# An MLP whose work is ordered by a list scheduler written in the kernel, in place of the framework's scheduler

## The chip, the cores and the metric

The kernel runs on one core of a Trainium2 chip. The metric is the device time of one launch in microseconds (us), median of the runs.

## What is computed

Sigmoid attention over 4 batches of 12 heads (448 tokens, 64 channels), then two MLP layers over all 1792 tokens (768 channels, 2048 hidden); weights arrive as 64-bit floats.

```python
scores = scale * np.matmul(q, k.transpose(0, 1, 3, 2)) - np.log(S)
attn = 1.0 / (1.0 + np.exp(-scores))
x = np.matmul(attn, v)               # to [1792, 768]
h = x @ w_in;  r = np.maximum(h, 0.0);  x = (r * r) @ w_out
h = x @ w_in2; x = (np.maximum(h, 0.0) + alpha * np.minimum(h, 0.0)) @ w_out2
```

## The kernel before

After the attention, the MLP runs as 32 **units** `(layer, p, fp)`: two layers, two pairs of batches (896 tokens), eight pairs of 128 hidden channels. Every fp32 operand is split into a high and a low part, and three matmuls (high-high, high-low, low-high) make one product.

A unit has an inward half and an outward half. Inward, seven products in Winograd's way (`product`, line 389; 9 matmuls of 448 columns each, so 63) go to three PSUM banks `h0` to `h2`, in the order 0, 1, 2, 1, 2, 0, 1. Products 3, 4 and 6 add on to a bank whose earlier sum VectorE must have read (`add`, line 581, into tiles `c12`, `c22`, `c21`). ScalarE and VectorE then make the hidden values `g` (`hidden`, line 397: squared ReLU in layer 0, leaky ReLU in layer 1). Outward (`out_products`, line 435), six pairs of outputs in layer 0 or seven in layer 1, with 12 matmuls each, 72 of 448 or 84 of 384 columns, go in turn to two double banks `o0` and `o1`; `collect` (line 457) adds each pair to `acc` on VectorE (line 468; ScalarE at line 466 where `fp` is 0). A pair needs the bank of the pair before the last.

Beside this, each unit prepares the next ones. For the weights, `load` brings a 64-bit block to one of two `raw` buffers, `scale` (ScalarE, lines 94 and 96) and `join` (VectorE, line 103) make a 32-bit one in `words_i` or `words_o`, or in place, which is also kept in DRAM (line 105) and recalled for the second pair of batches (line 111). `weight_sum` and `weight_parts` make the inward operands `wi`; `out_parts` and `out_low` (ScalarE line 494, GpSimd line 498) make the outward operands `wo` from `words_o`, of which there is one buffer. For the other pair of batches, `x_sums` and `wait_in_dram` prepare its inputs on GpSimd through one buffer `stage`, which a DMA empties to DRAM (line 504).

The attention stands in `tc.manual_schedule()`, which keeps the program's order. The MLP stands behind it. There, the program only says at which step a job is put (`at("i0", ...)`), and the framework's scheduler orders all engines by its own estimates, TensorE too. Each engine executes its queue in order.

Of the kernel before, what the change touches and what calls it, by code (L numbers as in the profile page):

```python
# [16 lines left out]
P = 128  # L17


@with_exitstack  # L20
def fused_kernel(ctx: ExitStack, tc: tile.TileContext, q, k, v, w1i, w1o, w2i, w2o, alpha, out):
# [14 lines left out]
    nc = tc.nc  # L36
# [33 lines left out]
    words = {kind: wpool.tile([P, 2, DM], F32, name=f"words_{kind}") for kind in "io"}  # L70
    late = dpool.tile([P, NC * PAIR], F32, name="late")
# [4 lines left out]
    raws = {}  # L76

    def load(n, kind, j):
# [4 lines left out]
        raw = raws[n, kind, j] = wpool.tile([P, DM, 2], I32, tag="raw", name=f"raw{n}{kind}{j}", bufs=2)  # L83
        d = raw.rearrange("p m t -> p (m t)").bitcast(I64)
# [5 lines left out]
    def scale(n, kind, j, word):  # L90

        half = raws[n, kind, j][:, :, word]
# [5 lines left out]
    def join(n, kind, j):  # L98

        raw = raws.pop((n, kind, j))  # L100
        layer, p, fp = UNITS[n]
        to = words[kind][:, j].bitcast(I32) if layer == 0 else raw.rearrange("p m t -> p (m t)")[:, :DM]
        nc.vector.scalar_tensor_tensor(out=to, in0=raw[:, :, 1], scalar=3, in1=raw[:, :, 0], op0=ALU.logical_shift_left, op1=ALU.bitwise_or)
        keep = kept[layer, 2 * fp + j, kind] = dpool.tile([P, DM], F32, name=f"kept{n}{kind}{j}")
        nc.sync.dma_start(out=keep, in_=to.bitcast(F32))

    def recall(n, kind):

        layer, p, fp = UNITS[n]
        for j in range(2):  # L110
            nc.sync.dma_start(out=words[kind][:, j], in_=kept[layer, 2 * fp + j, kind])

    def turn_of(n):

        return n if n < NB else n + NB

    def weight_sum(i, eng=None):
# [3 lines left out]
        eng = eng or nc.vector  # L121
# [10 lines left out]
    def weight_parts(what):  # L132

        first, w = {"a1": (0, words["i"][:, 0]), "a2": (2, words["i"][:, 1, HALF:]), "s12": (3, sums[:, :2 * HALF]), "s34": (5, sums[:, 2 * HALF:])}[what]
        hi, lo = (W[:, i, first * HALF:first * HALF + w.shape[-1]] for i in range(2))
        nc.scalar.activation(hi, w, AF.Copy)  # L136
        nc.vector.tensor_sub(lo, w, hi)  # L137
# [6 lines left out]
    def blocks(p):  # L144
        a = values_of(p)
        return ([a[:, kh * KH + c, t] for c in range(KH)] for kh, t in ((0, 0), (0, 1), (1, 0), (1, 1)))

    def x_sums(p, i, c, eng):
        b11, b12, b21, b22 = blocks(p)
        to, x, y = ((b12, b12, b11), (b12, b22, b12), (b11, b12, b11), (b12, b21, b12))[i]  # L150
        eng.tensor_sub(to[c], x[c], y[c])  # L151


    def x_parts(p, i, c, eng, to=None):
        b11, b12, b21, b22 = blocks(p)
        x = (b11, b12, b12, b11, b22, b21, b12)[i][c]
        hi, lo = to or (X[i][:, 0, c], X[i][:, 1, c])
        nc.scalar.activation(hi, x, AF.Copy)  # L158
        eng.tensor_sub(lo, x, hi)  # L159
# [4 lines left out]
    with tc.manual_schedule():  # L164
# [6 lines left out]
        with tc.tile_pool(name="apool", bufs=1) as apool, tc.tile_pool(name="apsum", bufs=1, space=bass.MemoryType.PSUM) as psum:  # L171
# [139 lines left out]

            ready_x = []
            for what in X_ORDER[:-1]:
                make = x_sums if what[0] == "s" else x_parts
                ready_x += [lambda i=int(what[1]), c=c, make=make: make(0, i, c, either()) for c in range(KH)]
            for d in range(ND):
# [17 lines left out]
                if d in (2, 3):  # L334
                    load(*early[d - 2])
                if item:
                    scale(*item, 1)
                    scale(*item, 0)
# [15 lines left out]
                if item:  # L354
                    join(*item)
                if 0 <= i < 4:
                    load(*early[i + 2])
# [14 lines left out]
    mpool = ctx.enter_context(tc.tile_pool(name="mpool", bufs=1, reuse_waits="tile"))  # L372
    psum = ctx.enter_context(tc.tile_pool(name="mpsum", bufs=1, space=bass.MemoryType.PSUM, reuse_waits="tile"))
    X.append(mpool.tile([P, 2, KH, S], F32R, name="x6"))
    e21, e22, e12, e11 = (mpool.tile([P, S], F32, name=f"c{s}") for s in ("21", "22", "12", "11"))
    pos = [mpool.tile([P, S], F32, name=f"pos{i}") for i in range(2)]
    WO = [mpool.tile([P, 2, DM], F32R, name=f"wo{j}") for j in range(2)]
    G = [mpool.tile([P, 2, PAIR], F32R, name=f"g{j}") for j in range(2)]
    acc.append(mpool.tile([P, NC * PAIR], F32, name="acc1"))
    stage = mpool.tile([P, 2, S], F32R, name="stage")  # L380
    two = [psum.tile([P, 2, 512], F32, name="o0")]
    hb = [psum.tile([P, 512], F32, name=f"h{i}") for i in range(3)]
    two.append(psum.tile([P, 2, 512], F32, name="o1"))
    BANK = (0, 1, 2, 1, 2, 0, 1)
    OPERAND = (0, 4, 3, 5, 6, 1, 2)
    HIGH, LOW = ((0, 0), (0, 1)), ((1, 0),)
    turns = {"pair": 0, "pos": 0, "x": 0}

    def product(k):

        ps = hb[BANK[k]][:, :S]
        for c in range(KH):
            at = OPERAND[k] * HALF + c * P
            for i, (wp, xp) in enumerate(((0, 0), (0, 1), (1, 0))):
                nc.tensor.matmul(ps, W[:, wp, at:at + P], X[k][:, xp, c], start=(k < 3 and c == 0 and i == 0), stop=(c == KH - 1 and i == 2), skip_group_check=True)  # L395

    def hidden(n, src, e, j, t):

        layer, p, fp = UNITS[n]
        gh, gl = (G[j][:, i, t * S:(t + 1) * S] for i in range(2))  # L400
        if layer == 0:
            nc.scalar.activation(e, src, AF.Relu)  # L402
            nc.scalar.activation(gh, e, AF.Square)  # L403
            nc.scalar.activation(e, e, AF.Square)  # L404
            second = lambda: None
        else:
            f = 2 * fp + j
            up = pos[turns["pos"] % 2]
            turns["pos"] += 1
            nc.scalar.activation(up, src, AF.Relu)  # L410
            nc.scalar.activation(e, src, AF.Relu, scale=-1.0)  # L411

            def second():
                nc.vector.scalar_tensor_tensor(out=e, in0=e, scalar=nal[:, f:f + 1], in1=up, op0=ALU.mult, op1=ALU.add)  # L414
                nc.scalar.activation(gh, e, AF.Copy)  # L415
        return second, lambda: nc.vector.tensor_sub(gl, e, gh)  # L416

    def outputs(n):

        if UNITS[n][0] == 0:  # L420
            return [[(c, t), (c + 1, t)] for t in (1, 0) for c in range(0, NC, 2)]
        return [[(m, 0), (m, 1)] for m in reversed(range(NM))]

    def out_product(n, o, ps, j, ways, begin, end):

        for i, (gi, wi) in enumerate(ways):
            if UNITS[n][0] == 0:
                c, t = o
# [223 lines left out]
```

## Time and profile before

| | |
|---|---|
| median of 3 runs | 1110.5 us (1109.63 to 1111.69) |
| the profiled execution, own time | 1106.94 us |
| its span, first to last instruction | 1105.2 us |
| TensorE busy, matmul / weight load | 1057.4 us (96%) / 911.7 us (82%) |
| VectorE, ScalarE, GpSimd busy | 764.2, 587.4, 271.6 us |
| mean granted TensorE clock | 0.993 |

PE is TensorE's matmuls, PEld its weight loads, DVE VectorE, ACT ScalarE, POOL GpSimd, SP the queue that issues DMAs. Matmuls overlap: one lasts 0.36 us in the records while the next starts 0.2 us after it. Idle time before an instruction, and what ended it, stands in brackets in a timeline.

### The profile page before, as it was taken

The page shows a single profiled execution, that of the slowest core. Times are in us where ns is not written, and L with a number is a line of the kernel's source. Part 1 is how long each engine was busy: PE and PEld are TensorE (multiplying, and loading weights), DVE is VectorE, ACT ScalarE, POOL GpSimd, SP SyncE. Part 2 cuts the span into 40 slices and gives each one's busy share as a digit, 9 for nine tenths or more (in the row PEclk, how much of TensorE's full clock was granted, in tenths as well). Part 3 has the DMA queues.
Part 4 walks back from the last instruction along what each step waited for, and adds up shares of the span by engine and source line. Part 5 has one row for each costly group of instructions (what it writes and reads, how often), then busy time and mean ns, then how long its engine had stood idle before and what let it go on. Part 6 is the DMA issues. An engine that isn't in the chain of part 4 may idle for free.

```text
span 1105.2 us, 14871 instructions
## 1 busy us (share of the span) xinstructions
PE 1057.4 (96%) x5607; PEld 911.7 (82%) x5607; DVE 764.2 (69%) x990; ACT 587.4 (53%) x933; POOL 271.6 (25%) x229
## 2 busy tenths in 40 slices
PE   9999899999999989999999989899999999999998
PEld 5555458888888878887889878899999999999997
DVE  5556967677777785777677674666666756666664
ACT  4567667665555667666656435433333553333332
POOL 0011224354311151543211156411111211111110
PEclk9999899999999999999999999999999999999999
DMA  7577827456654677687766533322112922121103
GB/s 151 143 196 197 238 85 269 172 197 221 221 172 156 229 272 247 236 272 239 250 227 214 217 142 111 126 72 60 58 59 56 334 71 59 58 58 59 57 26 101
DMA packets 126008, 174.79 MB, mean 158 GB/s; under 512 B 55536, under 2 KB 98800, under 8 KB 124272
## 3 DMA queue, kind: packets, MB, share of 16 engines
q1 hardware_dynamic: 123440, 172.59, 48.6%
q10 hardware_dynamic: 2496, 1.25, 0.4%
q8 instruction: 44, 0.72, 0.3%
q14 instruction: 28, 0.23, 0.1%
HBM read 123.87 MB, written 49.94 MB: 157 GB/s over the span
## 4 chain that ended last, share of the span: by engine, by line
PE 52%; issue 13%; DMA 11%; ACT 10%; POOL 8%; DVE 5%; SPq 0%; ACTq 0%; POOLq 0%; DVEq 0%
PE o L433 24%; PE h L395 18%; PE av L265 4%; POOL wo L498 4%; PE sc L245 3%; DMA kept_x<-stage 3%; POOL stage L159 2%; ACT wi L136 1%; POOL acc L151 1%; POOL x L159 1%; ACT c L404 1%; ACT c L402 1%; DVE acc L468 1%; ACT g L403 1%; PE scr L255 1%
## 5 line engine op out<-in xcount | busy, mean ns | idle before, releaser
L395 PE MATMUL h<-x,wi 128*128 128x448 f32 x2016 | 429.4, 368 | 16.8 <-DVE c L581 12.5
L395 PEld LDWEIGHTS h<-x,wi 128*128 128x128 f32 x2016 | 376.3, 188 | 59.3 <-DVE c L581 19.0
L433 PE MATMUL o<-g,wo 128*128 128x448 f32 x1152 | 245.0, 369 | 14.4 <-DVE acc L468 11.8
L498 POOL TENSOR_TENSOR wo<-words_o,wo 128x384 fp32r<-128x384 f32 x128 | 138.7, 1115 | 461.9 <-ACT wo L494 461.9
L433 PEld LDWEIGHTS o<-g,wo 128*128 128x128 f32 x1152 | 214.8, 189 | 41.1 <-DVE acc L468 19.0
L433 PE MATMUL o<-wo,g 128*128 128x384 f32 x1344 | 241.6, 337 | 7.1 <-ACT g L415 5.8
L433 PEld LDWEIGHTS o<-wo,g 128*128 128x128 f32 x1344 | 235.1, 189 | 10.9 <-ACT g L415 6.6
L468 DVE TENSOR_TENSOR acc<-o,acc 128x768 f32<-128x768 f32 (+1 forms) x182 | 184.2, 1015 | 58.0 <-PE o L433 57.2
L581 DVE TENSOR_TENSOR c<-h,c 128x448 f32<-128x448 f32 x160 | 99.1, 620 | 108.3 <-PE h L395 96.3
L494 ACT ACTIVATE wo<-words_o 128x768 fp32r<-128x768 f32 x64 | 51.0, 838 | 168.7 <-PE o L433 132.5
L416 DVE TENSOR_TENSOR g<-c,g 128x448 fp32r<-128x448 f32 x128 | 80.5, 644 | 30.6 <-ACT c L404 29.4
L247 ACT ACTIVATE a<-sc,bias 128x896 f32<-128x896 f32 x72 | 69.1, 1003 | 32.1 <-PE av L265 19.2
L159 POOL TENSOR_TENSOR stage<-acc,stage 128x448 fp32r<-128x448 f32 x36 | 48.1, 1335 | 150.7 <-ACT stage L158 150.7
L136 ACT ACTIVATE wi<-sums 128x768 fp32r<-128x768 f32 x64 | 53.6, 839 | 44.9 <-PE h L395 44.7
L137 DVE TENSOR_TENSOR wi<-sums,wi 128x768 fp32r<-128x768 f32 x64 | 69.0, 1081 | 7.4 <-ACT wi L136 6.5
L137 DVE TENSOR_TENSOR wi<-words_i,wi 128x768 fp32r<-128x768 f32 x64 | 52.5, 830 | 14.5 <-ACT wi L136 14.5
L151 POOL TENSOR_TENSOR acc<-acc 128x448 f32<-128x448 f32 x40 | 59.2, 1485 | 12.0 <-DVE acc L468 5.8
L265 PE MATMUL av<-a,v 128*64 128x448 f32 x288 | 61.7, 565 | 0.0
L158 ACT ACTIVATE stage<-acc 128x448 fp32r<-128x448 f32 x36 | 20.7, 574 | 66.3 <-DMA kept_x<-stage 53.2
L414 DVE SCALAR_TENSOR_TENSOR c<-c,nal,pos 128x448 f32<-128x448 f32 x64 | 43.5, 680 | 8.8 <-ACT c L411 8.6
L402 ACT ACTIVATE c<-c 128x448 f32<-128x448 f32 x48 | 27.3, 569 | 38.6 <-DVE c L581 38.6
L159 POOL TENSOR_TENSOR x<-acc,x 128x448 fp32r<-128x448 f32 x15 | 21.9, 1478 | 102.4 <-ACT x L158 102.4
(166 smaller groups left out, 943.7 us busy)
## 6 DMA issues: line engine op xcount, KB each, us to landing
kept_x<-stage SPq DMA_DIRECT2D x36, 448.0 KB, 3.4
x<-kept_x SPq DMA_DIRECT2D x12, 1344.0 KB, 10.1
v<-in_v_dram SPq DMA_DIRECT2D x24, 192.0 KB, 2.9
nat<-in_q_dram SPq DMA_DIRECT2D x22, 192.0 KB, 4.0
nat<-in_k_dram SPq DMA_DIRECT2D x20, 192.0 KB, 3.6
late<-held SPq DMA_DIRECT2D x12, 224.0 KB, 2.1
acc<-late SPq DMA_DIRECT2D x1, 2688.0 KB, 9.2
out_dram<-acc SPq DMA_DIRECT2D x14, 192.0 KB, 2.9
```

Of the source, the lines that this page charges most:

```text
L136: nc.scalar.activation(hi, w, AF.Copy)
L137: nc.vector.tensor_sub(lo, w, hi)
L151: eng.tensor_sub(to[c], x[c], y[c])
L159: eng.tensor_sub(lo, x, hi)
L247: nc.scalar.activation(sig[u, j], ps[:, :, :S], AF.Sigmoid, bias=bias[:, :1], scale=SCALE)
L265: nc.tensor.matmul(avs[u][h * D:(h + 1) * D, :S], vals[u][:, h, j, :], a[:, h, :], start=(u % 2 == 0 and j == 0), stop=(u % 2 == 1 and j = ...
L395: nc.tensor.matmul(ps, W[:, wp, at:at + P], X[k][:, xp, c], start=(k < 3 and c == 0 and i == 0), stop=(c == KH - 1 and i == 2), skip_group ...
L416: return second, lambda: nc.vector.tensor_sub(gl, e, gh)
L433: nc.tensor.matmul(ps, *ops, start=(begin and i == 0), stop=(end and i == len(ways) - 1), skip_group_check=True)
L468: nc.vector.tensor_add(part, both, part)
L498: nc.gpsimd.tensor_sub(WO[j][:, 1, at], words["o"][:, j, at], WO[j][:, 0, at])
L581: nc.vector.tensor_add(to, hb[bank][:, :S], other)
```

## The change

The whole MLP moves into `manual_schedule()`, and its work is no longer emitted where it is written. Each operation is added to a `Plan` with its engine, a duration, and keys for what it reads and writes. `Plan.run` places the operations in simulated time and emits them by their start. TensorE's operations keep the order in which they were added. Due times run back from TensorE's order; each other engine takes, among the operations that can begin, the one due first, unless it would delay a more urgent one that becomes ready meanwhile. VectorE operations that read two SBUF tiles and GpSimd's (`port=True`) are placed one at a time. DMAs are taken one after the other at 0.28 MB/us with 2 us on top.

The operations, their engines and their number stay as they were. `raw` becomes two fixed tiles, `join` loses its DMA to `keep`, and the recalls are one DMA each.

```diff
+class Plan:
+    HOP = 0.10
+    TAIL = {"PE": 0.17, "DVE": 0.085, "ACT": 0.095, "POOL": 0.04}
...
+    def run(self):
...
+        for j in pe:
+            due[j] = at
+            at += jobs[j][1]
+        for j in reversed(range(n)):
+            late = min((due[s] - self.HOP for s in after[j]), default=at + 50.0) - length(j) - self.TAIL.get(jobs[j][0], 0.0)
+            due[j] = min(due[j], late) if jobs[j][0] == "PE" else late
...
+        def begin(j, t):
+            t = max(t, ready[j])
+            return max(t, port_free) if jobs[j][4] else t
+        def choose(e):
+            queue = waiting[e]
+            if e == "PE":
+                queue = [j for j in queue if j == pe[next_pe]]
...
+            now = sorted((j for j in queue if begin(j, free[e]) <= t + 1e-9), key=lambda j: due[j])
+            soon = [j for j in queue if begin(j, free[e]) > t + 1e-9]
+            for j in now:
+                end = t + jobs[j][1]
+                if not any(due[s] < due[j] and begin(s, free[e]) < end and end > due[s] for s in soon):
+                    return t, j
...
+            if e == "SP" or size:
+                dma_free = max(dma_free, t + 0.1) + size / 0.28e6
+                end = dma_free + 2.0
...
+        for t, j in sorted(order):
+            jobs[j][2]()
...
+        def act(cols): return 0.10 + 0.00083 * cols
+        def dve(cols): return 0.07 + 0.00105 * cols
+        def pool(cols): return 0.13 + 0.0023 * cols
+        PE_IN, PE_OUT = 0.2005, (0.2005, 0.1735)
...
+            add("SP", 0.05, lambda: load(at, n, kind, j), [], [high, low], size=2 * DM * BYTES)
+            add("ACT", act(DM), lambda: scale(at, 1), [high], [high])
+            add("ACT", act(DM), lambda: scale(at, 0), [low], [low])
+            add("DVE", dve(DM), lambda: join(at, n, kind, j), [high, low], to, port=True)
...
-        step(0)
-        nc.scalar.activation(e21, hb[0][:, :S], AF.Copy)
-        do("i0")
...
+            add_inward(n)
...
+            add_outward(n)
+        plan.run()
```

Three places where the order moves. The numbers in names are buffers: in the rows of before `c_1789` is `c12`, `c_1788` `c22`, `c_1787` `c21`; in those of the change they are `c_1784`, `c_1783`, `c_1782`.

VectorE before, end of unit 2 and inward half of unit 3:

```order
L129 TENSOR_TENSOR sums<-words_i,sums 128x384
L468 TENSOR_TENSOR acc_76<-o_1803,acc_76 128x2x448
L103 SCALAR_TENSOR_TENSOR words_o<-raw4o_2469 128x768
L581 TENSOR_TENSOR c_1789<-h_1801,c_1787 128x448
L103 SCALAR_TENSOR_TENSOR words_o<-raw4o_2484 128x768
L581 TENSOR_TENSOR c_1788<-h_1802,c_1787 128x448
L137 TENSOR_TENSOR wi<-sums,wi 128x768
```

The same place in the change:

```order
L202 SCALAR_TENSOR_TENSOR words_o<-raw_82 128x768
L720 TENSOR_TENSOR acc_76<-o_1798,acc_76 128x2x448
L240 TENSOR_TENSOR wi<-words_i,wi 128x384
L202 SCALAR_TENSOR_TENSOR words_o<-raw_81 128x768
L720 TENSOR_TENSOR acc_76<-o_1794,acc_76 128x2x448
L720 TENSOR_TENSOR acc_76<-o_1798,acc_76 128x2x448
L662 TENSOR_TENSOR c_1784<-h_1796,c_1782 128x448
L202 SCALAR_TENSOR_TENSOR words_i<-raw_82 128x768
L662 TENSOR_TENSOR c_1783<-h_1797,c_1782 128x448
```

The two joins into `words_o` leave the inward half for the outward half of the unit before; joins into `words_i`, which nothing on GpSimd reads, stand among the adds.

TensorE before, outward half of unit 1, second and third pair:

```order
L433 MATMUL o_1799<-g_1795,wo_1793 128x448 x6
L433 MATMUL o_1803<-g_1795,wo_1793 128x448 x6
L395 MATMUL h_1800<-x_70,wi 128x448
L433 MATMUL o_1799<-g_1795,wo_1793 128x448 x3
L433 MATMUL o_1799<-g_1796,wo_1794 128x448 x3
```

The same place in the change:

```order
L534 MATMUL o_1794<-g_1790,wo_1788 128x448 x6
L534 MATMUL o_1798<-g_1790,wo_1788 128x448 x6
L534 MATMUL o_1794<-g_1790,wo_1788 128x448 x3
L534 MATMUL o_1794<-g_1791,wo_1789 128x448 x3
L534 MATMUL o_1794<-g_1790,wo_1788 128x448 x3
```

The matmuls of the next unit's first product, one to five per unit, no longer stand between the second and third pair.

ScalarE before, end of unit 16 and inward half of unit 17:

```order
L494 ACTIVATE wo_1793<-words_o 128x768
L466 ACTIVATE acc_76<-o_1799 128x768
L494 ACTIVATE wo_1794<-words_o 128x768
L587 ACTIVATE c_1787<-h_1800 128x448
L158 ACTIVATE stage<-acc_1797 128x448
L136 ACTIVATE wi<-sums 128x768
L158 ACTIVATE stage<-acc_1797 128x448
L410 ACTIVATE pos_1791<-c_1788 128x448
```

The same place in the change:

```order
L628 ACTIVATE wo_1788<-words_o 128x768
L628 ACTIVATE wo_1789<-words_o 128x768
L718 ACTIVATE acc_76<-o_1794 128x768
L669 ACTIVATE c_1782<-h_1795 128x448
L190 ACTIVATE raw_82<-raw_82 128x768
L192 ACTIVATE raw_82<-raw_82 128x768
L261 ACTIVATE stage<-acc_1792 128x448
L236 ACTIVATE wi<-sums 128x768
L650 ACTIVATE pos_1786<-c_1783 128x448
```

One write of `stage` is left in the inward half, ahead of the first hidden value; the next one comes in the outward half.

## Rows read from the trace of the kernel before

**Rows 1.** Stretches: busy us (count) of PE, PEld, DVE, ACT, POOL; clock; DMA share; GB/s.

```profile
164.30:649.10 484.80, 453.63 (x2166) 403.08 (x2165) 358.06 (x429) 290.55 (x475) 157.44 (x121) 1.00 0.65 221
649.10:713.70 64.60, 57.95 (x295) 53.87 (x294) 37.52 (x50) 31.64 (x56) 33.35 (x29) 0.97 0.35 120
713.70:1105.20 391.50, 386.65 (x2057) 368.73 (x2055) 261.46 (x380) 158.94 (x279) 60.31 (x60) 1.00 0.26 82
428.40:431.80 3.40, 3.40 (x10) 2.80 (x10) 2.02 (x3) 3.40 (x6) 0.00 (x0) 0.50 0.49 146
```

**Rows 2.** Lines 395 and 433: ns min/median/max, first and last start in us.

```profile
L395 PEld LDWEIGHTS h<-x,wi x2016: 186/188/338, 164.3 to 1085.4; 128*128 128x128 f32 x184
L395 PE MATMUL h<-x,wi x2016: 360/368/659, 164.3 to 1085.6; 128*128 128x448 f32 x184
...
L433 PE MATMUL o<-wo,g x1344: 333/334/525, 663.3 to 1100.5; 128*128 128x384 f32 x192
```

**Rows 3.** Timeline of PE, a unit of layer 1: start us, us busy.

```profile
952.11 0.56 PE L395 MATMUL h<-x,wi 128*128 128x448 f32 x2
...
979.68 0.57 PE L395 MATMUL h<-x,wi 128*128 128x448 f32 x2
```

**Rows 4.** Timeline of PE, a unit of layer 0.

```profile
317.53 12.77 PE L395 MATMUL h<-x,wi 128*128 128x448 f32 x62
330.14 3.13 PE L433 MATMUL o<-g,wo 128*128 128x448 f32 x14
...
337.56 9.99 PE L433 MATMUL o<-g,wo 128*128 128x448 f32 x48 [0.95 <-DVE acc L468]
347.39 0.97 PE L395 MATMUL h<-x,wi 128*128 128x448 f32 x4
```

**Rows 5.** Waits of PE from 164 us on: total us, times, longest.

```profile
PE h L395 <- DVE c L581: 12.5, 14, 2.1
PE o L433 <- DVE acc L468: 12.3, 14, 2.1
PE o L433 <- ACT g L415: 5.8, 2, 4.3
PE h L395 <- ACT wi L136: 3.5, 3, 2.0
PE o L433 <- DVE g L416: 2.2, 5, 0.8
```

**Rows 6.** Timeline of unit 3, inward half.

```profile
257.98 4.66 POOL L498 TENSOR_TENSOR wo<-words_o,wo 128x384 fp32r<-128x384 f32 x4 [2.41 <-ACT wo L494]
...
260.01 1.76 DVE L103 SCALAR_TENSOR_TENSOR words_o<-raw4o 128x768 int32<-128x768 int32 x1 [1.56 <-POOL wo L498]
...
261.70 0.61 DVE L581 TENSOR_TENSOR c<-h,c 128x448 f32<-128x448 f32 x1
...
262.37 2.09 PE L395 MATMUL h<-x,wi 128*128 128x448 f32 x9 [1.11 <-DVE c L581]
...
265.16 5.75 PE L395 MATMUL h<-x,wi 128*128 128x448 f32 x27 [0.70 <-DVE c L581]
```

**Rows 7.** Timeline of unit 17, ScalarE and PE.

```profile
693.04 0.58 ACT L158 ACTIVATE stage<-acc 128x448 fp32r<-128x448 f32 x1 [7.04 <-DMA kept_x<-stage]
...
697.02 5.31 PE L433 MATMUL o<-wo,g 128*128 128x384 f32 x20 [4.25 <-ACT g L415]
```

**Rows 8.** Timeline of DVE, the unit of rows 3, adds of the first two pairs.

```profile
951.31 1.95 DVE L468 TENSOR_TENSOR acc<-o,acc 128x768 f32<-128x768 f32 x2
```

**Rows 9.** Joins of one unit, and all adds of line 468: ns min/median/max.

```profile
L103 DVE SCALAR_TENSOR_TENSOR words_o<-raw7o x2: 957/1360/1764, 350.2 to 352.9; 128x768 int32<-128x768 int32 x2
...
L468 DVE TENSOR_TENSOR acc<-o,acc x182: 944/958/1092, 213.5 to 1100.9; 128x768 f32<-128x768 f32 x98, 128x896 f32<-128x896 f32 x84
```

**Rows 10.** DMA issues from 180 to 390 us: count, KB each, median us to landing.

```profile
kept_x<-stage SPq DMA_DIRECT2D x12, 448.0 KB, 6.1
...
raw5o<-in_moe_w_out_dram SPq DMA_DIRECT2D x2, 768.0 KB, 6.7
```

More of the change, by code (lines that the diff above doesn't have):

```diff
@@ L70, in fused_kernel, with load @@
     words = {kind: wpool.tile([P, 2, DM], F32, name=f"words_{kind}") for kind in "io"}
+    raw = [wpool.tile([P, DM, 2], I32, name=f"raw{i}") for i in range(2)]
     late = dpool.tile([P, NC * PAIR], F32, name="late")
     kept = {}
-    raws = {}
-    def load(n, kind, j):
+    def load(at, n, kind, j):
         layer, p, fp = UNITS[n]
@@ L378, in fused_kernel @@
[L378 to L426, printed above, removed]
-            if UNITS[n][0] == 0:
-                c, t = o
-                ops = WO[j][:, wi, c * P:(c + 1) * P], G[j][:, gi, t * S:(t + 1) * S]
-            else:
-                m, e = o
-                ops = G[j][:, gi, m * P:(m + 1) * P], WO[j][:, wi, e * HALF:(e + 1) * HALF]
-            nc.tensor.matmul(ps, *ops, start=(begin and i == 0), stop=(end and i == len(ways) - 1), skip_group_check=True)
@@ new lines, in fused_kernel, with product, outputs @@
+        CELL = 64
+        def product(k):
+            ps = hb[BANK[k]][:, :S]
+            for c in range(KH):
+                at = OPERAND[k] * HALF + c * P
+                for i, (wp, xp) in enumerate(((0, 0), (0, 1), (1, 0))):
+                    nc.tensor.matmul(ps, W[:, wp, at:at + P], X[k][:, xp, c], start=(k < 3 and c == 0 and i == 0), stop=(c == KH - 1 and i == 2), skip_group_check=True)
+        def outputs(n):
+            if UNITS[n][0] == 0:
+                return [[(c, t), (c + 1, t)] for t in (1, 0) for c in range(0, NC, 2)]
+            return [[(m, 0), (m, 1)] for m in reversed(range(NM))]
@@ new lines, in sides, with out_product @@
+        def sides(n, o):
+            if UNITS[n][0] == 0:
+                return [o[1]]
+            return [t for t in range(2) if o[0] * P < (t + 1) * S and (o[0] + 1) * P > t * S]
+        def out_product(n, o, ps, j, ways, begin, end):
+            for i, (gi, wi) in enumerate(ways):
+                if UNITS[n][0] == 0:
+                    c, t = o
+                    ops = WO[j][:, wi, c * P:(c + 1) * P], G[j][:, gi, t * S:(t + 1) * S]
+                else:
+                    m, e = o
+                    ops = G[j][:, gi, m * P:(m + 1) * P], WO[j][:, wi, e * HALF:(e + 1) * HALF]
+                nc.tensor.matmul(ps, *ops, start=(begin and i == 0), stop=(end and i == len(ways) - 1), skip_group_check=True)
@@ new lines, in fused_kernel, with act, dve, pool @@
+        plan = Plan()
+        add = plan.add
+        def act(cols):
+            return 0.10 + 0.00083 * cols
+        def dve(cols):
+            return 0.07 + 0.00105 * cols
+        def pool(cols):
+            return 0.13 + 0.0023 * cols
+        PE_IN, PE_OUT = 0.2005, (0.2005, 0.1735)
+        BYTES = 4 * P
+        def cells_of(p, name, c):
+            kh, t = PLACE[name]
+            return [("acc", p, ((kh * KH + c) * 2 + t) * S // CELL + k) for k in range(S // CELL)]
+        def add_x_sum(p, i, c, engine):
+            to, x, y = X_SUM[i]
+            add(engine, pool(S) if engine == "POOL" else dve(S), lambda: x_sum(p, i, c, nc.gpsimd if engine == "POOL" else nc.vector), cells_of(p, x, c) + cells_of(p, y, c), cells_of(p, to, c), port=True)
@@ new lines, in add_out_weights, with low @@
+        def add_out_weights(n):
+            def low(j, e):
+                at = slice(e * HALF, (e + 1) * HALF)
+                nc.gpsimd.tensor_sub(WO[j][:, 1, at], words["o"][:, j, at], WO[j][:, 0, at])
+            for j in (1, 0):
+                add("ACT", act(DM), lambda j=j: nc.scalar.activation(WO[j][:, 0], words["o"][:, j], AF.Copy), [("words", "o", j)], [("wo", j, 0)])
+            for j in (1, 0):
+                for e in range(2):
+                    add("POOL", pool(HALF), lambda j=j, e=e: low(j, e), [("words", "o", j), ("wo", j, 0)], [("wo", j, 1, e)], port=True)
```

491 lines of the change are left out of this document (287 added, 204 removed).

## The prediction

> **What bounds the kernel now.** I read the stretches first, to see where TensorE is not full. From 713.7 us on PE is busy for 386.65 of 391.5 us; from 164.3 to 649.1 us, which is units 0 to 15 (layer 0), only for 453.63 of 484.8, and from 649.1 to 713.7 us for 57.95 of 64.6 [rows 1]. VectorE, the fullest of the others, is busy for 358.06 of the 484.8 us there. So no engine but PE is full, and yet PE waits: that is a matter of order, and it lies in layer 0 and in units 16 and 17.
>
> A matmul's record overlaps the next one, so what PE could do is counted from start to start. A unit of layer 1 repeats after 979.68 - 952.11 = 27.57 us [rows 3] with no wait listed. In layer 0, 62 inward matmuls take 330.14 - 317.53 = 12.61 us, 0.2034 each, and 48 outward ones 347.39 - 337.56 = 9.83, 0.2048 each [rows 4]; 63 x 0.2034 + 72 x 0.2048 = 27.56 us. All 32 units back to back are 882.2 us. The MLP's matmuls run from 164.3 to 1100.5 us, the last one 0.33 more [rows 2]: 936.5 us. The **excess is 54.3 us**, and no order of the same work gains much more than that.
>
> Then the waits of PE. The five pairs listed make 12.5 + 12.3 + 5.8 + 3.5 + 2.2 = 36.3 us in 38 waits [rows 5]. Each costs more than its idle time: the wait of 0.95 us [rows 4] follows a matmul whose record lasts 0.37 [rows 2], so the two starts stand 1.32 us apart instead of 0.20: 1.12 us lost, 0.16 more than the idle time. That makes 38 x 0.16 = 6.1 us. The granted clock is 0.50, which is 1.2 GHz, from 428.4 to 431.8 us, and 0.97 on average from 649.1 to 713.7 us [rows 1], the stretch that holds the longest wait, 4.25 us [rows 7]. Ten matmuls in 3.4 us where 0.204 us each would make 16.7 is 1.4 us lost; 3% of 64.6 is 1.9. Together 36.3 + 6.1 + 3.3 = 45.7 us; 8.6 us of the excess are in gaps that this view does not list.
>
> **How much PE has to gain is read differently from two rows.** The idle time of PE in units 0 to 15 is 484.8 - 453.63 = 31.2 us [rows 1], while by starts it is 484.8 - 16 x 27.56 = 43.8. I go by starts. The Trainium skill says on its page Perfetto Trace Analysis, section Identifying the Most-Contended Engine, that matmul busy time flatters a kernel because matmuls are pipelined, and that the busy share of the weight loads is to be taken. By that rule, with 0.188 us a load and 0.204 a start, 403.08 us of loads fill 437 us, and the stretch would have 48 us to give instead of 31; this trace agrees with the rule.
>
> **The change, part by part.** It adds and removes no operation, so everything is a shift.
>
> *Joins into words_o leave the inward half.* In unit 3 the first stands at the head of VectorE's queue from 258.45 to 260.01 us, because GpSimd is still reading the one buffer, and the add that PE needs is behind it: 261.70, and PE goes on at 262.37 after 1.11 us; the same once more with 0.70 us [rows 6]. In the change both joins stand in the outward half of the unit before, ahead of GpSimd's reads, and the adds follow each other with one join into words_i between them. That removes the reason for most waits on line 581, and the other part of the change should take the rest: 12.5 + 14 x 0.16 = 14.7 us. What hides the moved joins is the outward half: with 0.96 us each when GpSimd is quiet they fit between two adds of line 468, which last 1.09 [rows 9] and come every 12 x 0.2048 = 2.46 us [rows 4].
>
> *Halves of `wi`, hidden values and adds of pairs are put in order of need.* Waits on line 468 and 416 go where VectorE was busy with something less urgent: 14.5 + 19 x 0.16 = 17.5 us. Waits on `wi` (3.5 us, 3 times [rows 5]) I put down to the next unit's matmuls, which the framework moved ahead of the end of a unit; that is no longer done: 4.0 us.
>
> *ScalarE.* In unit 17 it stood 7.04 us before the write of `stage`, whose DMA was under way, with unit 17's first hidden value behind it; PE then waited for 4.25 us [rows 7]. Now one write of `stage` is left there and the other comes behind the hidden values: 5.8 + 2 x 0.16 = 6.1 us, and the clock's 3.3 us come back with it.
>
> *What the change takes away.* In the unit of rows 3, pair 3 needs the bank that pair 1 leaves. VectorE's add of pair 1 begins at 951.31 and lasts 0.96, so until 952.27 [rows 8, 9]; pair 2's matmuls are over at 952.11 [rows 3]. Before, two matmuls of the next unit stood in this hole. Now PE waits there in each unit: 0.16 us and the way of a semaphore, which I take as 0.2. In layer 0 the add lasts 1.09 us [rows 9] against six matmuls of 0.205 us, so about the same; the four units with `fp` 0 use ScalarE and I leave them out. 28 x 0.2 = **5.6 us given back**, some of it in layer 1, which has no wait today. Bounds: 0, if the add is quicker by the wait, and 0.95 + 0.16 us a unit as in rows 4, which is 31 us, if VectorE comes late. I take the low end since the order puts nothing that waits for a DMA ahead of that add in the units that I followed.
>
> *SP's queue.* The loads, keeps and recalls move against each other, each by a few us. Their cover is a unit's slack; the third rival is what happens without it.
>
> *GpSimd and the port.* A join into words_o took 0.96 us at its quickest and up to 1.76 beside GpSimd's reads, while the adds of line 468, which read PSUM, never took over 1.09 [rows 9]. The planner keeps the two apart only as far as its durations hold: it reckons 0.88 us for a join. I allow half of the unlisted 8.6 us, 4.3, for what stays of this.
>
> **Sum.** 54.3 - 5.6 - 4.3 = 44.4 us. From the profiled execution's 1106.94 us that leads to 1062.5; the median of the runs stands 3.6 us above that execution, so 1110.5 - 44.4 = **1066 us**.
>
> **The rivals.**
> 1. *Half of it.* VectorE still comes late by a port conflict or by durations that are too short (0.88 us planned for 0.96 to 1.76 [rows 9]). For: VectorE and GpSimd together have 358 + 157 = 515 us of work in 484.8 us [rows 1], so they must overlap. Against: the adds on PSUM, a good part of it, need no turn [rows 9]. At half of 54.3 us the time is 1083.
> 2. *All of it.* The hole between pairs 2 and 3 closes, or the planner's order hides it, and nothing else is late: 1110.5 - 54.3 = 1056.
> 3. *Slower: DMAs land later than the planner believes, and block ScalarE.* It reckons 786,432 bytes as 2.8 + 2.0 = 4.8 us and `stage` as 3.6, one after the other; here they took 6.7 and 6.1 us [rows 10]. ScalarE's `scale` or `stage` then stands at the head of its queue, 1.9 and 2.5 us late, with hidden values behind. Units 0 to 14 load and 17 to 22 write `stage`; if each of those 21 lost both, that is 92 us, less 54.3: 1149. It turns the sign from 54.3 / 21 = 2.6 us a unit. Against: the first hidden value has slack. Its sum can be read when product 3 ends, 36 x 0.2034 = 7.3 us into a unit [rows 4]; an add of 0.61 [rows 6] and two ScalarE operations of about 0.58 [rows 7] make it ready at 9.1, and PE asks for it at 63 x 0.2034 = 12.8 us.
> 4. *The change does not do what it says.* The order shows TensorE's products without the framework's shifts, so this needs a second reordering that I do not see.
>
> **How the numbers follow.** The forecast has 0.68, half of it 0.15, all of it 0.09, slower 0.05, nothing 0.03. A measurement of this kernel tells about 0.2%, 2.2 us, from no change. Faster by more: 0.92. Within: 0.03. Slower: 0.05. The range goes from 1057, next to all of it, to 1084, which takes in half of it; what lies outside is part of the second case, the third and the fourth.
>
> **What would show it.** PE's waits for the adds of line 581's successor, for `wi` and for the hidden values should be gone, and the clock 1.00 from 164 us on. One short wait of about 0.2 us for the add of pair 1 should appear in nearly every unit, in layer 1 too, so that its units take 27.8 us instead of 27.57. VectorE's joins into words_o should no longer wait for GpSimd. The prediction is wrong if units 0 to 15 take over 29 us each, if a wait of ScalarE for a DMA comes with one of PE, or if layer 1 slows by more than 0.5 us a unit.

## The result and the profile after

The changed kernel takes **1071.34 us** (median of 4 runs, 1070.24 to 1072.4), the kernel before 1111.1 beside it: ratio 0.964, with 95% between 0.9615 and 0.9662. The forecast was 1066 and 1057 to 1084. The profiled execution took 1072.4 us with a span of 1070.2; it is compared here with the 1106.94 and 1105.2 of before. That execution of the kernel before was about 4 us quicker than the median of its runs, and this one 1.1 us slower than its own, so the traces show 34.5 us of the 39.8 by which the medians differ.

The stretches of the changed kernel: the attention, layer 0, layer 1 (columns as in [rows 1]):

```profile
5.60:158.30 152.70, 151.70 (x1085) 81.89 (x1083) 104.04 (x126) 103.78 (x123) 19.26 (x14) 1.00 0.66 168
158.30:616.80 458.50, 447.99 (x2162) 405.44 (x2161) 322.06 (x420) 296.19 (x462) 135.71 (x119) 1.00 0.64 219
616.80:1066.00 449.20, 446.49 (x2353) 421.56 (x2351) 309.87 (x443) 207.02 (x348) 96.41 (x90) 1.00 0.31 105
```

And the attention of the kernel before:

```profile
5.60:164.30 158.70, 154.93 (x1086) 82.58 (x1084) 106.77 (x130) 104.75 (x123) 19.81 (x14) 0.98 0.66 171
```

So the 35.0 us of span come from three places: **6.0 from the attention**, 26.3 from layer 0 (484.8 us in [rows 1], 458.5 now) and 2.6 from layer 1 (from 649.1 us to the end of the last matmul, 1100.8 [rows 2], 451.7, and 449.1 now, to 1065.9); the rest is rounding, as 4.3 us lie behind the last matmul in both. In layer 1, units 16 and 17 took 30.5 and 34.1 us before and take 27.8 and 28.7 now, while most of the others have become slower. VectorE was busy in layer 0 for 358.06 us [rows 1] and now for 322.06. Nine operations, eight of them joins, have left the stretch, some 8 us by an estimate from 0.95 us a join; the rest is that operations beside GpSimd's were long, and now fewer do: a half of `wi` from `sums` took 1.14 us on average there and now takes 0.95.

TensorE's waits in the MLP now, to be set against [rows 5]:

```profile
PE o L534 <- DVE acc L720: 11.0, 25, 2.4
...
PE h L511 <- DVE c L662: 0.4, 1, 0.4
```

Line 662 is the old 581, 720 the old 468. The waits for the adds of the inward half are gone but one, those for `wi` and for ScalarE's hidden values too. What is left is nearly one kind: 25 waits for the add of a pair; the other rows of this view make 1.6 us.

The joins (line 103 before, 202 now): VectorE's idle time before them, from the start of the MLP to 400 us, first before, then after:

```profile
  POOL wo L498: 18.2, 13
```

```profile
L202 DVE SCALAR_TENSOR_TENSOR words_o<-raw x14: 941/950/1373, 168.1 to 358.0; 128x768 int32<-128x768 int32 x14
...
  ACT raw L192: 7.8, 3
```

13 joins had waited for GpSimd; none does now, and the median join into words_o takes 0.95 us, where 11 of the 14 had taken over 1.75.

A unit of layer 1 now, on PE and on VectorE (the unit of rows 3 took 27.57 us):

```profile
953.78 13.18 PE L511 MATMUL h<-x,wi 128*128 128x448 f32 x63
...
971.30 10.69 PE L534 MATMUL o<-wo,g 128*128 128x384 f32 x60 [0.17 <-DVE acc L720]
981.83 0.36 PE L511 MATMUL h<-x,wi 128*128 128x448 f32 x1
```

```profile
969.82 0.56 DVE L240 TENSOR_TENSOR wi<-words_i,wi 128x384 fp32r<-128x384 f32 x1
970.29 1.83 DVE L720 TENSOR_TENSOR acc<-o,acc 128x768 f32<-128x768 f32 x2
```

It takes 28.05 us. The wait is 0.17 us, near the 0.2 that was forecast, but it costs 28.05 - 27.57 = 0.48 us: in the trace the two starts around it stand 0.51 us apart and the next two 0.28, where 0.17 is usual.

The longest wait left is in unit 3; first VectorE, then PE, and the clock:

```profile
262.93 0.62 DVE L654 TENSOR_TENSOR g<-c,g 128x448 fp32r<-128x448 f32 x1 [0.73 <-ACT c L644]
263.47 2.08 DVE L720 TENSOR_TENSOR acc<-o,acc 128x896 f32<-128x896 f32 x2
```

```profile
264.61 4.68 PE L534 MATMUL o<-g,wo 128*128 128x448 f32 x14 [2.38 <-DVE acc L720]
```

```profile
265.03:268.44 3.41, 3.41 (x11) 3.02 (x10) 1.85 (x3) 2.67 (x5) 0.66 (x1) 0.50 0.02 5
```

VectorE stands idle ahead of the low half of a hidden value, waiting for ScalarE, and the add that PE needs is behind it. The clock fell to 0.50 (1.2 GHz) after this wait of 2.38 us, and after none of the shorter ones in the MLP.

**Two things were not in the forecast.** The first is in the attention. ScalarE and PE before, then ScalarE after:

```profile
129.36 0.88 ACT L94 ACTIVATE raw1o<-raw1o 128x768 f32<-128x768 f32 x1 [5.06 <-DMA raw1o<-in_moe_w_out_dram]
...
130.94 0.98 ACT L247 ACTIVATE a<-sc,bias 128x896 f32<-128x896 f32 x1
```

```profile
131.98 0.74 PE L245 MATMUL sc<-qkh 64*128 64x448 f32 x2 [2.81 <-ACT a L247]
```

```profile
126.38 1.01 ACT L352 ACTIVATE a<-sc,bias 128x896 f32<-128x896 f32 x1 [2.05 <-PE av L370]
127.28 0.90 ACT L190 ACTIVATE raw<-raw 128x768 f32<-128x768 f32 x1
```

The framework had moved a scale operation of the MLP (unit 1's w_out) up into the attention, ahead of a sigmoid, where it waited 5.06 us for its DMA. PE's wait of 2.81 us ended at 131.98 us, and the clock stood at 0.50 from 131.5 to 138.0 us. The planner starts where the attention's code ends, so the sigmoid now comes first.

The second is ScalarE's time for a hidden value (relu, square, square in place; lines 402 to 404 before, 642 to 644 now). Before, two values stood interleaved; now one value's operations follow each other:

```profile
301.56 0.54 ACT L402 ACTIVATE c<-h 128x448 f32<-128x448 f32 x1
301.99 1.04 ACT L403 ACTIVATE g<-c 128x448 fp32r<-128x448 f32 x2
302.92 1.04 ACT L404 ACTIVATE c<-c 128x448 f32<-128x448 f32 x2
```

```profile
460.39 0.56 ACT L642 ACTIVATE c<-c 128x448 f32<-128x448 f32 x1
460.98 0.58 ACT L643 ACTIVATE g<-c 128x448 fp32r<-128x448 f32 x1
461.59 0.58 ACT L644 ACTIVATE c<-c 128x448 f32<-128x448 f32 x1
```

Two pairs start 0.93 us apart there, 0.47 an operation; here the starts are 0.59 and 0.61 us apart. An operation that needs its own engine's last result, or overwrites what the last one reads, starts 0.03 us after that record ends; one that does neither starts 0.1 us before. The Trainium skill, page Perfetto Trace Analysis, section Per-instruction lifecycle, says as much: the next instruction may begin to fetch when the one before has finished executing in the engine, while the semaphore is given only when the write is acknowledged, which is the end of the record. These rows agree. The planner reckons 0.47 us in both cases. What came of it in this unit, on VectorE and PE:

```profile
462.20 0.62 DVE L654 TENSOR_TENSOR g<-c,g 128x448 fp32r<-128x448 f32 x1 [0.52 <-ACT c L644]
462.75 2.08 DVE L720 TENSOR_TENSOR acc<-o,acc 128x896 f32<-128x896 f32 x2
```

```profile
463.88 2.33 PE L534 MATMUL o<-g,wo 128*128 128x448 f32 x10 [0.51 <-DVE acc L720]
```

### The profile page after: what moved, and what is told of

The parts are those of the page before. It is cut to its first block, busy times and chain, and to the rows that moved or that the text cites. A ratio compares the mean times of both kernels' runs of the same rounds, so it can differ in the third digit from the quotient of the medians.

```text
span 1070.2 us, 14822 instructions
## 1 busy us (share of the span) xinstructions
PE 1050.4 (98%) x5607; PEld 912.3 (85%) x5607; DVE 737.3 (69%) x990; ACT 608.5 (57%) x933; POOL 252.1 (24%) x229
## 3 DMA queue, kind: packets, MB, share of 16 engines
q10 hardware_dynamic: 2496, 1.25, 0.4%
## 5 line engine op out<-in xcount | busy, mean ns | idle before, releaser
L511 PE MATMUL h<-x,wi 128*128 128x448 f32 x2016 | 419.9, 367 | 0.5 <-DVE c L662 0.4
L625 POOL TENSOR_TENSOR wo<-words_o,wo 128x384 fp32r<-128x384 f32 x128 | 128.8, 1038 | 416.6 <-ACT wo L628 369.3
L662 DVE TENSOR_TENSOR c<-h,c 128x448 f32<-128x448 f32 x160 | 99.6, 623 | 164.6 <-PE h L511 160.6
L264 POOL TENSOR_TENSOR stage<-acc,stage 128x448 fp32r<-128x448 f32 x36 | 45.3, 1258 | 183.2 <-ACT stage L261 183.2
L236 ACT ACTIVATE wi<-sums 128x768 fp32r<-128x768 f32 x64 | 53.3, 837 | 48.1 <-PE h L511 30.5
L190 ACT ACTIVATE raw<-raw 128x768 f32<-128x768 f32 x64 | 57.8, 904 | 16.0 <-DMA raw<-in_moe_w_in_dram 11.5
L240 DVE TENSOR_TENSOR wi<-sums,wi 128x768 fp32r<-128x768 f32 x64 | 61.0, 956 | 5.9 <-ACT wi L236 5.6
L370 PE MATMUL av<-a,v 128*64 128x448 f32 x288 | 59.4, 548 | 0.0
L192 ACT ACTIVATE raw<-raw 128x768 int32<-128x768 uint32 x64 | 57.6, 900 | 0.0
L650 ACT ACTIVATE pos<-c 128x448 f32<-128x448 f32 x48 | 27.8, 578 | 51.1 <-DVE c L662 50.2
L257 POOL TENSOR_TENSOR acc<-acc 128x448 f32<-128x448 f32 x40 | 53.6, 1348 | 11.4 <-DMA acc<-late 9.5
L240 DVE TENSOR_TENSOR wi<-words_i,wi 128x768 fp32r<-128x768 f32 x64 | 50.1, 786 | 6.6 <-ACT wi L236 4.7
```

What stands on the lines that cost most here:

```text
L190: nc.scalar.activation(half.bitcast(F32), half.bitcast(F32), AF.Prelu, scale=2.0 ** -112, alpha=2.0 ** 32)
L192: nc.scalar.activation(half, half.bitcast(U32), AF.Copy, scale=2.0 ** -29 * (1 - 2.0 ** -12), bias=-0.5 + 7.5 * 2.0 ** -12)
L370: nc.tensor.matmul(avs[u][h * D:(h + 1) * D, :S], vals[u][:, h, j, :], a[:, h, :], start=(u % 2 == 0 and j == 0), stop=(u % 2 == 1 and j = ...
L625: nc.gpsimd.tensor_sub(WO[j][:, 1, at], words["o"][:, j, at], WO[j][:, 0, at])
L662: add("DVE", dve(S), lambda: nc.vector.tensor_add(to, bank(b), other), [("h", b), other_key], [key])
```

## The experiments

**1. The written order, without framework and without planner.** The kernel before, its MLP put under the manual schedule by indenting it into that block, line for line:

```diff
-    mpool = ctx.enter_context(tc.tile_pool(name="mpool", bufs=1, reuse_waits="tile"))
+        mpool = ctx.enter_context(tc.tile_pool(name="mpool", bufs=1, reuse_waits="tile"))
...
```

> The kernel before, with its MLP part under the manual schedule: the same statements, the same steps, issued in the order in which they are written, with neither the framework's scheduler nor the planner. Theory A (the due times earn the gain): the attention gets its 6.0 us back, since nothing of the MLP can be moved up into it, and the first MLP matmul stands at 158.3 us as in the changed kernel; but in the MLP the written order puts joins and halves ahead of the adds that TensorE needs, and the hole between pairs 2 and 3 is open (32 x 0.46 us), so the MLP takes longer than the 936.5 us of before and the whole is slower than before, 1115 to 1160 us. Rival B (the framework's moves did the harm, and any order without them does as well): within 10 us of the changed kernel, 1071 to 1081 us.

Measured: 1224.23 us, ratio 1.102 (1.1001 to 1.1044). The MLP starts at 158.9 us, so the attention's 6 us come with any order that leaves it alone. The MLP then takes 151 us more than in the changed kernel. TensorE's longest waits, and ScalarE in unit 5:

```profile
PE o L433 <- DVE acc L468: 44.0, 45, 2.3
PE h L395 <- DVE c L581: 33.9, 9, 7.4
```

```profile
326.01 0.58 ACT L158 ACTIVATE stage<-acc 128x448 fp32r<-128x448 f32 x1 [3.42 <-DMA kept_x<-stage]
```

Theory A holds, by more than its range. The framework's order was not bad: it had earned 113 us over the written one. Here the third rival of the prediction is at work: ScalarE waits at `stage` for a DMA, with the work that PE needs behind. VectorE then stands idle for 6.72 us ahead of its next add, which needs ScalarE, until 327.82 us, and PE waits for that add for 3.82.

**2. The one scale operation put back into the attention.**

```diff
+                    if d == 9 and j == R - 1:
+                        scale(0, 1)
+                        scale(0, 0)
                     scores(u, j)
...
+                if i == 4:
+                    load(0, 1, "o", 0)
```

> The changed kernel, with one load and its two scale operations (the first block of w_out of unit 1) taken from the plan and put where the framework had moved them: the load behind the join that frees its buffer, the scales on ScalarE ahead of the third sigmoid of the tenth double step of the attention. Theory A (that one placement cost the 6.0 us of the attention): ScalarE waits about 5 us for the DMA, TensorE about 2.8 us behind it, the granted clock is 0.5 for about 6.8 us, and the MLP starts at 164.3 instead of 158.3 us: 1077 us. Rival B (the 6.0 us came from the sums and other work that the framework also moved into the attention): ScalarE's wait is there, but the MLP starts before 160 us: 1071 to 1073 us.

Measured: 1076.2 us, ratio 0.968 (0.9658 to 0.9706).

```profile
133.04 0.88 ACT L190 ACTIVATE raw<-raw 128x768 f32<-128x768 f32 x1 [8.11 <-DMA raw<-in_moe_w_out_dram]
```

```profile
135.66 0.74 PE L350 MATMUL sc<-qkh 64*128 64x448 f32 x2 [5.12 <-ACT a L352]
```

The wait, PE's wait and the clock (0.50 from 134 to 140 us) come back, larger than before since the DMA landed later; the MLP starts at 167.5 us, and its 32 units, re-planned, take 3 us less. Theory A, with the start of the MLP missed by 3 us.

**3. Two matmuls more between pair 1 and pair 3.**

```diff
-            for ways in (HIGH, LOW):
-                for os, b in pairs[:2]:
+            for ways, some in ((HIGH, pairs[:2]), (LOW, pairs[:1])):
+                for os, b in some:
...
             for at, (os, b) in enumerate(pairs):
+                if at == 1:
+                    for i in range(2):
+                        products(os, b, i, 1, LOW, False, False)
```

> The changed kernel with TensorE's order of the outward half changed by four matmuls: the last factor of j = 1 of pair 2 comes after pair 1 is complete, so that 8 matmuls instead of 6 stand between the end of pair 1 and pair 3. Theory A (the hole between pairs 2 and 3 gives back 0.46 us a unit in layer 1 and about 0.7 in layer 0): two matmuls are 0.35 us in layer 1 and 0.41 in layer 0, and the refill of 0.1 us goes with the wait. Layer 1's units take 27.6 instead of 28.04 us, layer 0's about 0.4 us less: 14 x 0.45 + 14 x 0.4 = 12 us less than the changed kernel, 1059 us. Rival B (VectorE sets the pace there, or the halves that pair 1 now needs two matmuls earlier come late): the wait moves to the hidden values, to the halves of wo or to a later pair, and no more than 4 us are gained: 1067 us or more.

Measured: **1058.25 us**, ratio 0.953 (0.9507 to 0.9551).

```profile
PE o L534 <- DVE acc L723: 3.1, 6, 1.0
```

Theory A, 13 us where 12 were expected. The rest of PE's waits makes 2.0 us, about as much as in the changed kernel, so none moved elsewhere.

**4. A price for results of the same engine.**

```diff
+    SELF = {"DVE": 0.11, "ACT": 0.14}
...
-                ready[s] = max(ready[s], t + us if jobs[s][0] == e and e != "SP" else end + self.HOP)
+                ready[s] = max(ready[s], t + us + self.SELF.get(e, 0.0) if jobs[s][0] == e and e != "SP" else end + self.HOP)
```

> The changed kernel with one more price in the planner: an operation that needs the result of the one before it on its own engine is ready 0.14 us (ScalarE) or 0.11 us (VectorE) later than the planner believed. In the changed kernel's trace ScalarE's second and third operation of a hidden value start 0.59 and 0.61 us after the one before, where the planner reckons 0.47; in the trace of before, where two hidden values stand interleaved, they start 0.467 us apart. Theory A (the planner is late in layer 0 because it takes those chains for 0.27 us a hidden value too short, and puts VectorE's last low half, which waits for ScalarE, ahead of the add of pair 1): the waits of TensorE on the add of pair 1 in layer 0 shrink to about the 0.2 us that they have in layer 1, the wait of 2.4 us in unit 3 goes with its clock, and the time falls by 4 to 7 us: 1064 to 1067 us. Rival B (the lateness comes from DMAs or from the port shared with GpSimd, which this price does not touch): within 2 us of the changed kernel.

Measured: 1059.36 us, ratio 0.954 (0.9517 to 0.9556), 12 us less than the changed kernel. TensorE's waits for adds of pairs, the same add in the unit of line 462.75 above, and a unit of layer 1:

```profile
PE o L535 <- DVE acc L721: 0.9, 3, 0.6
```

```profile
455.82 2.31 DVE L721 TENSOR_TENSOR acc<-o,acc 128x896 f32<-128x896 f32 x2 [0.91 <-PE o L535]
458.04 1.32 DVE L655 TENSOR_TENSOR g<-c,g 128x448 fp32r<-128x448 f32 x1
```

```profile
942.13 13.18 PE L512 MATMUL h<-x,wi 128*128 128x448 f32 x63
...
970.02 1.19 PE L512 MATMUL h<-x,wi 128*128 128x448 f32 x5
```

VectorE now stands ready when pair 1 ends, and the low half comes behind the adds. Theory A, and more than its 4 to 7 us: the missing price had made VectorE late in nearly all units, not in unit 3 alone. The edit prices ScalarE and VectorE at once; what each is worth wasn't measured. A unit of layer 1 takes 27.89 us, so of its 0.48 above, 0.16 was lateness and 0.32 the hole as such. No wait is listed there any more, but the starts around the hole still stand 0.34 and 0.28 us apart instead of 0.17: a wait that the last record covers isn't listed, and costs all the same.

**5. Both.** The edits of experiments 3 and 4.

> The two edits of e3_reorder and e4_selfdep together. Theory A (they close two different things: the price brings VectorE in time, which leaves a hole of 0.17 us of waiting in layer 1 and about 0.13 in layer 0, and the four moved matmuls close that): all 32 units take 27.6 to 27.9 us, 32 x 27.7 + 158.3 + 6 = 1051 us of span, 1052 to 1055 us. Rival B (both edits buy the same slack, each is enough): within 1 us of the better of the two, 1057 to 1059 us.

Measured: **1050.25 us**, ratio 0.945 (0.9412 to 0.9481), the best kernel here, 21 us below the changed one. PE in layer 0, then in layer 1:

```profile
435.25 12.93 PE L512 MATMUL h<-x,wi 128*128 128x448 f32 x63
...
462.61 12.93 PE L512 MATMUL h<-x,wi 128*128 128x448 f32 x63
```

```profile
933.18 13.18 PE L512 MATMUL h<-x,wi 128*128 128x448 f32 x63
...
960.76 0.57 PE L512 MATMUL h<-x,wi 128*128 128x448 f32 x2
```

Units of 27.36 and 27.58 us without a wait: theory A, 2 us below its range. Ten of the 16 units of layer 0 take 27.36; units 0 to 5 still take 27.5 to 28.2, and unit 17 takes 30.3. The two edits share 4 us (12 + 13 against 21).

**6. The two matmuls of the next unit put back into the hole.**

```diff
+                if at == 1 and n + 1 < NU:
+                    add("PE", AHEAD * PE_IN, lambda: product(0, 0, AHEAD), [("w", "a1", 0), *x_keys(0, 0)], [("h", 0)])
...
```

`AHEAD` is 2. Unit n + 1's first product then begins with its third matmul, and its words_i enter the plan before unit n's outward half.

> The changed kernel with what the framework had done between pairs 2 and 3 put back by hand: the first two matmuls of the next unit's first product stand there (0.41 us), for which the next unit's words_i and its high half of a1 enter the plan before the outward half. Theory A (the removed matmuls are the only reason for the hole): in layer 1 the wait of 0.17 us and its refill go, 0.46 us in 14 units, and in layer 0 about 0.41 us in 13 units: 1071 - 12 = 1059 us. Rival B (the earlier need for a1 moves VectorE's and ScalarE's work so that waits for a1 or for the hidden values take their place): 1066 us or more.

Measured: 1059.72 us, ratio 0.952 (0.9485 to 0.9559).

```profile
PE o L537 <- DVE acc L726: 6.9, 10, 1.5
```

Theory A's time, within 1 us, but not its "only reason": ten waits for adds of pairs stay, 6.9 us. The framework's shift of matmuls into this hole, which the change gave up, was worth about 12 us when put back with two.

**7. First come, first served in place of due times.**

```diff
-            now = sorted((j for j in queue if begin(j, free[e]) <= t + 1e-9), key=lambda j: due[j])
+            now = sorted((j for j in queue if begin(j, free[e]) <= t + 1e-9), key=lambda j: j)
...
-                if not any(due[s] < due[j] and begin(s, free[e]) < end and end > due[s] for s in soon):
+                if not any(s < j and begin(s, free[e]) < end and end > due[s] for s in soon):
```

> The changed kernel with the planner's choice by due times replaced by the order in which the jobs are added (the earlier job first, and an engine is held only for an earlier job); durations, dependences and port stay. Theory A (the due times are what orders halves, hidden values and adds by need): the halves and joins of the next unit are added before the hidden values and the adds of this one, so they go first whenever they are ready, and TensorE waits for adds and hidden values as in the kernel before or more: 1095 to 1130 us. Rival B (any planner that knows the durations and keeps VectorE from idling does it): within 6 us of the changed kernel, 1065 to 1077 us.

Measured: 1089.14 us, ratio 0.979 (0.9755 to 0.9823), between the theories.

```profile
PE o L534 <- DVE acc L720: 22.5, 20, 2.7
```

Known durations and dependences already beat the framework by 23 us, 6 of which are the attention's and come without any planner (experiment 1); the choice by due times is worth the other 18. One use of them is left in this run, `end > due[s]` in the last line, so it is not wholly a planner without them.

**8. No regard for the shared port.**

```diff
-            return max(t, port_free) if jobs[j][4] else t
+            return t
```

> The changed kernel with a planner that no longer holds VectorE and GpSimd apart: it starts both whenever they are free. Theory A (the planner's rule for the shared port buys little, as VectorE's order in time is what counts): 1068 to 1074 us, joins of 1.9 us and longer stand beside GpSimd's work in the trace. Theory B (the rule is a good part of layer 0's gain, and my forecast's allowance of 4.3 us for what stays of the port is the lower end): VectorE's operations that meet GpSimd's last up to 1.8 us instead of 0.95, adds come late, and the time rises by 5 to 20 us: 1076 to 1091 us.

Measured: 1087.56 us, ratio 0.977 (0.9742 to 0.9807): theory B, 16 us, 13 of it in layer 0 (471.6 us against 458.5). TensorE's waits for the adds of the inward half, back again, one of VectorE's sums beside GpSimd (0.55 us when alone), and layer 0 as a whole:

```profile
PE h L511 <- DVE c L662: 8.1, 6, 2.0
```

```profile
223.25 1.25 DVE L222 TENSOR_TENSOR sums<-sums,words_i 128x384 f32<-128x384 f32 x1
```

```profile
221.78 4.89 POOL L625 TENSOR_TENSOR wo<-words_o,wo 128x384 fp32r<-128x384 f32 x4 [5.92 <-ACT wo L628]
```

```profile
158.80:630.40 471.60, 450.97 (x2163) 407.64 (x2162) 341.20 (x423) 299.47 (x465) 146.13 (x120) 0.99 0.65 219
```

VectorE is busy for 341 us instead of 322 with nearly the same work (423 operations against 420). The adds of pairs, which have one operand in PSUM, still never take over 1.09 us. The Trainium skill, page SBUF — State Buffer, section Who interferes with whom, has the rule: an operation of VectorE with two SBUF inputs and one of GpSimd that reads SBUF exclude each other for a whole instruction; one with at most one SBUF input, outside VectorE's two-port modes, is free of it. The trace agrees on both: 1.25 us for the sum, and never over 1.09 for the adds.

**9. The joins put back ahead of the adds.** Unit n + 1's w_out enters the plan before unit n's inward half, and the add of product 3 (and likewise of 4) waits for a join:

```diff
-                    total(e22, 1, e22, "e22", "e22")
+                    total(e22, 1, e22, "e22", "e22", *([("words", "o", 0)] if n + 1 < NB else []))
```

> The changed kernel with the joins into words_o put back ahead of two adds of the inward half: unit n + 1's blocks of w_out enter the plan before unit n's inward half, and the add of product 3 must stand behind the join of the first block, the add of product 4 behind that of the second, for n from 0 to 6. A join must wait until GpSimd has read the buffer, so the adds wait too. Theory A (my term for the joins, 14.7 us, is right in kind): TensorE's waits on these adds return, in 7 units, about 1 us for the first and 0.7 for the second as in rows 6, with 0.16 each on top: 7 x 2.0 = 14 us, 1085 us. Rival B (TensorE's wait for the adds was due to the other halves on VectorE, not to the joins): under 4 us more than the changed kernel, up to 1075 us.

Measured: 1076.79 us, ratio 0.968 (0.9656 to 0.9697), 5 us over the changed kernel, with intervals that touch. In unit 3, GpSimd and VectorE:

```profile
245.39 5.33 POOL L625 TENSOR_TENSOR wo<-words_o,wo 128x384 fp32r<-128x384 f32 x4 [3.95 <-ACT wo L628]
```

```profile
250.61 2.78 DVE L202 SCALAR_TENSOR_TENSOR words_o<-raw 128x768 int32<-128x768 int32 x2
253.31 1.14 DVE L662 TENSOR_TENSOR c<-h,c 128x448 f32<-128x448 f32 x2
```

PE has no wait for line 662 in this run, and no join stands idle for GpSimd. Neither theory as written: a join ahead of the adds is harmless where GpSimd's reads start early enough to be over by then. In [rows 6] they started at 257.98 and the join stood waiting. That state didn't come back here, so what the joins cost in it isn't measured. In the profiled execution (1073.55 us, 3 below the median) units 0 to 6, where the joins were moved, take 199.2 us against 202.4 in the changed kernel, and unit 17 takes 32.7 against 28.7: what was lost lies elsewhere.

**10. A planner that believes in slower DMAs,** otherwise experiment 5:

```diff
-            return jobs[j][1] if jobs[j][0] != "SP" else jobs[j][5] / 0.28e6 + 2.0
+            return jobs[j][1] if jobs[j][0] != "SP" else jobs[j][5] / 0.2e6 + 2.5
...
```

> The kernel of e5_both, with a planner that reckons its DMAs slower: 786,432 bytes as 3.9 + 2.5 = 6.4 us instead of 4.8, one of stage as 4.8 instead of 3.6, nearer to the 5.1 to 6.7 and 3.5 to 6.1 us of the traces. Theory A (third rival of the prediction wrong in kind: ScalarE waits for DMAs, but the hidden values have slack): within 2 us of e5_both. Theory B (late DMAs are part of what is left): ScalarE's waits for stage and raw shrink, and the time falls by 2 to 4 us.

Measured: 1094.29 us, ratio 0.984 (0.9819 to 0.9861): 44 us worse than experiment 5, and neither theory. SP's queue, and PE:

```profile
819.82 0.32 SPq L776 DMA_DIRECT2D x<-kept_x  x1
832.01 0.32 SPq L214 DMA_DIRECT2D words_i<-kept17i  x1
832.37 0.43 SPq L214 DMA_DIRECT2D words_o<-kept23o  x1
```

```profile
837.44 0.69 PE L535 MATMUL o<-wo,g 128*128 128x384 f32 x1 [10.41 <-ACT wo L629]
```

Most units of layer 0 run at 27.36 us and most of layer 1 at 27.58, but in three units the other durations made PE wait for weights: units 8, 22 and 23 take 39.1, 34.5 and 48.6 us, 40 us too much. Above, a recall whose buffer is still in use stands ahead of one that PE needs, and SP stands at it for 12 us. Elsewhere the slower durations did good: units 0 to 5 take 164.6 us against 167.5 in experiment 5, and unit 17 takes 27.6 against 30.3, 5.6 us that speak for theory B. The profiled execution took 1086 us, the others up to 1095. Why the planner, reckoning with these durations, chose that order was not followed up.

## Why the prediction was right, and where not

**The floor and the excess** were right in kind. Experiment 5 reaches 27.36 us in ten units of layer 0, so the 27.56 of the prediction was 0.2 too high there, 3 us over 16 units.

**Joins, halves, hidden values, `stage`:** the waits on which these terms rest are gone, 12.5 us for the adds of the inward half down to 0.4. The reason given for the joins was right (GpSimd still reading), the remedy only half: that they left the inward half matters less than that they no longer meet GpSimd, as experiments 8 and 9 show. No run prices the 14.7 us of this term by itself.

**The adds of pairs** did not go as forecast. Their waits were most of the 17.5 us that the order of need was to bring; they were 12.3 us in 14 waits [rows 5] and are 11.0 in 25. Most of what is left is the add of pair 1, which the next step is about.

**"28 x 0.2 = 5.6 us given back" is the step that failed.** The MLP's matmuls now run from 158.32 to 1066 us, 25.4 over the 882.2, where 5.6 + 4.3 = 9.9 were left for them. The term was too small: closing the hole and bringing VectorE in time together give 21 us (experiment 5). In layer 1 the size is off by the prediction's own rule: it had found that a wait costs 0.16 us more than its idle time, and did not charge that here; 0.32 us measured in experiment 4. In layer 0 the bound at the high end, 1.11 us a unit "if VectorE comes late", was the truer one: 458.5 / 16 = 28.66 us a unit, 1.30 over the 27.36 of experiment 5. The reason for taking the low end, that nothing waiting for a DMA stands ahead of that add, looked at the wrong wait: what stood ahead of it waited for ScalarE: in nine units of layer 0, the two above among them, VectorE is idle for 0.3 to 0.7 us ahead of a low half shortly before that add.

**"Durations that are too short"** were named in the first rival, but as those of joins beside GpSimd. What was too short is the chain of ScalarE, by 0.27 us a hidden value; with a price for it and for VectorE's chains the kernel is 12 us quicker (experiment 4).

**The port:** 4.3 us was allowed for what stays of it. That remainder wasn't measured by itself; that the planner's rule for it is worth 16 us was (experiment 8).

**The attention** was taken as unchanged. That 6 us lay there was to be seen in the trace of before, in a wait of PE at 131.98 us and the clock behind it; the prediction read PE's waits only from 164 us on. This miss hides a part of the other: 15.5 us too much were to be recovered in the MLP, 6.0 elsewhere were not seen. The sum for the profiled execution was 1062.5, and 1072.4 came. The medians, 1066 and 1071.34, stand closer still, only because the profiled execution of before was a quick one. That the forecast lies 5 us off and not 15 is luck.

**What was to show it:** the 0.2 us wait is there in eleven of layer 1's 16 units (0.17 to 0.29 us). Its units became 0.48 us slower, where 0.5 would have been a sign against the prediction, and units 0 to 15 take 28.66 us on average, where 29 would have been one. That the clock would be 1.00 from 164 us on failed in unit 3 alone. Of the rivals, the third is real in mechanism (experiment 1; experiment 10 shows loads that wait in SP's own queue) but doesn't set the time of this order.

## What to carry to other kernels

A scheduler that reckons with durations is as good as the prices that it leaves out: here the wait of an operation for its own engine's last result was worth 12 us, the shared port 16, the choice by due times 18, each taken by itself; such gains overlap. When a framework's scheduler is taken away, list what it did well: two matmuls in a hole were worth 12 us, and four matmuls in another order 13. Read the trace beyond the code that the change touches: moved work had cost 6 us in a stage that the diff leaves alone.

## What the runs showed of the hardware

- On ScalarE, 448 columns follow each other after 0.47 us when independent, after 0.59 to 0.61 when the second needs the first's result or overwrites what it reads.
- The clock went to 0.50 (1.2 GHz) at waits of PE of, among others, 2.38 us (changed kernel), 5.12 (experiment 2) and 1.97, 2.81 and 4.25 (kernel before; the first is the stretch from 428.4 us in [rows 1]). It stayed at 1.00 behind waits of 2.06, 2.09 and 2.14 us in the kernel before and behind those of 0.85 us or less in the MLP of the changed kernel. The length of a wait alone doesn't tell.
- SP takes its DMAs in order: a recall stood 11.9 us for its buffer, and the next one, which PE needed, stood behind it; PE waited for 10.41 us (experiment 10).
